# Filling free slots by scatter, moving the first weights, and reordering the tail of attention in a kernel of linear attention and two mixtures of experts

## The chip, the cores and the metric

The kernel runs on one core of a Trainium2 chip. The core has a matrix engine (TensorE, PE), a vector engine (VectorE, DVE), a scalar engine (ScalarE, ACT), a general engine (GpSimd, POOL) and a queue engine (SyncE, SP); each works through its own instructions in order, and semaphores tie them together. SP and POOL also issue the transfers (DMAs). The metric is the device time of one execution in microseconds (us); a kernel's time is the median of its runs.

## The reference

A linear attention with decay (4 batches, 8 heads, 768 steps, head size 48) makes 3072 tokens of width 384. A first mixture of 8 experts (hidden width 1024) sends each token through one expert; a second one does the same for the tokens whose skip score is positive and passes the others through.

```python
for t in range(S):                       # attention
    state = alpha[:, :, t, :, None] * state + einsum('bhd,bhe->bhde', k[:, :, t], v[:, :, t])
    y[:, :, t] = einsum('bhd,bhde->bhe', q[:, :, t], state)
...
e_idx = argmax(x @ w_gate, axis=1)       # first mixture, x: (3072, 384)
for e in range(E):
    mask = e_idx == e
    ye = maximum(x[mask] @ w1[e], 0.0) @ w2[e]
    out[mask] = gate_w[mask, None] * eom[mask, e, None] * ye
...
do_compute = x @ w_skip > 0              # second mixture
out[do_compute] = xc + gate_w[:, None] * (maximum(xc @ w1[e], 0.0) @ w2[e])
```

## The kernel before

**Attention.** The 3072 tokens are 24 chunks of 128 (tiles). A loop over i runs a list of steps (`stages`), each with a lag: at iteration i, a step with lag n works on chunk i + n. Steps of a chunk: `p_scan` (products of the decay along the chunk, DVE), `p_recip` (ACT), `p_k` and `p_q` (k and q scaled by them; the product t on POOL, the rest mostly on DVE), `scores` (PE), `mask` (DVE), `k_back` and `state` (the state S handed on), `y_of` (PE), `x_rows` (PE turns the result into rows of tokens, ACT copies them). The code order sets the order on each engine.

**Routing to experts.** After every four tiles (a group) `gate_logits` computes the gate's logits on PE, `x_route` picks the expert on DVE, and `x_place` ranks the tokens within their expert and writes each token's row (388 floats: 384 values, the weight, the token's number) with an indirect DMA of POOL (a scatter) into a scratch in memory, `scr1`. Expert e owns the rows from e * 3456 on. Groups 0 to 3 put their scatters into a list, from which `x_send` takes one per iteration; group 4's go at once; group 5 is routed and placed inside the first expert's layer 1.

**Free slots.** The first mixture reads 432 rows for every expert, however many tokens it has. So that free rows hold harmless values, `fill_region` (L137) writes a row of zeros with an out-of-range token number into all 432 rows of each expert first: four experts' fills are issued by SP inside the constants, the other four at the end of iteration 0. The scatters of tokens write over them. The constants themselves (`consts`, L111) run on POOL in the lead before the loop.

**Weights.** Each expert's weights come in six pieces of 128x1024, through a buffer of three (`load_piece`, L296). Each half of a piece is split into a high part (ACT, L307) and the rest (DVE, L308), since products are made of three terms. The first expert's pieces are loaded at iterations 4, 7, 10, 13, 16 and 19 and split at 7, 8, 10, 11 and so on to 23.

**Experts.** `stream` (L621) runs the items of `ITEMS` in turn. Item 0 is expert 0 with the rows present before the last group (early rows), item 1 the rest of expert 0, with the rows as the stationary side, items 2 to 8 are experts 1 to 7, and nine more items are the second mixture. An item's `layer1` (L403) makes eight blocks f of the hidden width, `layer2` (L450, L459) eight more; in layer 2 PE already transposes the next item's rows (L359). Steps of the item before (its own routing to `scr2` and its scatters), hooks, weight splits and the loading of the next item's rows (`load_rows`, L340) are woven in between the blocks. `bump` (L207) moves late tokens of expert 0 behind its early rows.

**The seam.** At iteration 22 SP loads expert 0's early rows into two buffers of the weight stage; `first_split`, called from `x_rows` of the last tile, transposes them (L359), splits them, and then the last group's logits follow (L286).

## Time and profile before

| | |
|---|---|
| Time, median of 3 runs (lowest to highest) | 584.15 us (583.17 to 587.17) |
| Profiled execution, its time | 584.72 us |
| Its span, first to last instruction | 582.5 us |
| Busy: PE, DVE, ACT, POOL | 94%, 64%, 53%, 28% |
| Attention (to the first layer 1) | 161.6 us |
| Mean granted clock of PE | 0.966 |

A row of a trace gives the start in us, the duration in us, the engine and line (SPq is SP's queue), the operation, and the tile written and the tiles read; x4 means four of them in a row, and then the duration covers all. In brackets stands how long the engine was idle before, and what ended that. A window's row gives busy time by engine; the share of DMA can pass 1 by a little, since packets overlap.

### The profile page before, as it was taken

What the parts mean: (1) busy time and instruction counts of PE and PEld (TensorE: products, weight loads), DVE (VectorE), ACT (ScalarE), POOL (GpSimd) and SP (SyncE); (2) the same over time, 40 slices, a digit from 0 to 9 for tenths busy, and PEclk for the clock granted to TensorE, in tenths of its full rate; (3) what the DMA queues carried; (4) which work ended last, traced back from release to release, by engine and by line L of the source; (5) the groups of instructions that cost most, each with busy time, mean ns of one, the idle gap of its engine ahead of it and who ended that gap; (6) DMA issues with size and microseconds to landing.
All of it is one profiled execution on the core that took longest, in us unless ns stands there. A gap on an engine that the chain in (4) does not pass through costs nothing.

```text
span 582.5 us, 11777 instructions
## 1 busy us (share of the span) xinstructions
PE 547.2 (94%) x4545; PEld 499.3 (86%) x4545; DVE 375.2 (64%) x867; ACT 309.2 (53%) x723; POOL 164.6 (28%) x171
## 2 busy tenths in 40 slices
PE   5995989897898999999999999999999999999995
PEld 4784777786698899999999999998997999999994
DVE  7997699998264463655546373745546786777850
ACT  3573666765443563645445464636465565566540
POOL 5334255554220320140606041231533011001111
PEclk9697898899889999999999999999999999999999
DMA  8989876331578335272635436162735757666610
GB/s 314 363 309 352 338 259 249 114 112 42 204 259 255 112 88 179 76 261 92 230 128 204 152 126 225 62 222 95 226 124 192 243 194 220 222 217 217 208 68 22
DMA packets 35949, 110.31 MB, mean 189 GB/s; under 512 B 6444, under 2 KB 13228, under 8 KB 35884
## 3 DMA queue, kind: packets, MB, share of 16 engines
q1 hardware_dynamic: 28940, 97.52, 49.0%
q0 software_dynamic: 6944, 11.96, 5.9%
q8 instruction: 37, 0.61, 0.4%
q14 instruction: 28, 0.23, 0.1%
HBM read 88.96 MB, written 27.13 MB: 199 GB/s over the span
## 4 chain that ended last, share of the span: by engine, by line
PE 68%; DVE 15%; DMA 8%; ACT 2%; POOL 2%; issue 2%; SPq 1%; POOLq 0%; DVEq 0%; ACTq 0%
PE ph L403 27%; PE py L450 17%; PE py L459 8%; PE py L403 3%; DVE A L947 3%; DVE P L892 3%; DMA st<-in_w1a_dram 2%; DVE r L917 2%; DMA st<-in_w2b_dram 2%; PE pt L359 2%; PE pt L489 2%; PE ph L421 2%; DVE k L919 1%; DVE qp L928 1%; DMA st<-in_w2a_dram 1%
## 5 line engine op out<-in xcount | busy, mean ns | idle before, releaser
L219 POOL DMA_INDIRECT scr<-x,pi x56 | 67.0, 1197 | 208.9 <-DVE ski L534 83.1
L403 PE MATMUL ph<-xh,w1h 128*128 128x432 f32 (+3 forms) x330 | 110.2, 334 | 0.0
L403 PE MATMUL ph<-xl,w1h 128*128 128x432 f32 (+3 forms) x330 | 106.6, 323 | 0.5 <-DVE xl L364 0.5
L403 PE MATMUL ph<-xh,w1l 128*128 128x432 f32 (+3 forms) x330 | 106.5, 323 | 0.0
L409 DVE SCALAR_TENSOR_TENSOR hl<-ph,hh 128x432 fp32r<-128x432 f32 (+3 forms) x110 | 56.2, 511 | 68.6 <-ACT hh L408 68.1
L308 DVE TENSOR_TENSOR w2l<-st,w2h 128x512 fp32r<-128x512 f32 x96 | 65.0, 694 | 42.9 <-ACT w2h L307 42.7
L408 ACT ACTIVATE hh<-ph 128x432 fp32r<-128x432 f32 (+3 forms) x110 | 50.1, 455 | 79.5 <-PE ph L403 79.3
L307 ACT ACTIVATE w2h<-st 128x512 fp32r<-128x512 f32 x96 | 58.2, 626 | 46.5 <-DMA st<-in_w2a_dram 25.6
L308 DVE TENSOR_TENSOR w1l<-st,w1h 128x512 fp32r<-128x512 f32 x96 | 63.2, 687 | 12.1 <-ACT w1h L307 9.5
L450 PE MATMUL py<-hh,w2h 128*128 128x432 f32 (+1 forms) x192 | 69.0, 359 | 0.0
L450 PE MATMUL py<-hh,w2l 128*128 128x432 f32 (+1 forms) x192 | 67.4, 351 | 0.0
L450 PE MATMUL py<-hl,w2h 128*128 128x432 f32 (+1 forms) x192 | 67.3, 350 | 0.0
L403 PEld LDWEIGHTS ph<-xh,w1h 128*128 128x128 f32 x330 | 62.7, 190 | 2.8 <-issue 1.6
L403 PEld LDWEIGHTS ph<-xl,w1h 128*128 128x128 f32 x330 | 62.5, 190 | 2.4 <-DVE xl L364 0.9
L403 PEld LDWEIGHTS ph<-xh,w1l 128*128 128x128 f32 x330 | 62.8, 190 | 1.1
L307 ACT ACTIVATE w1h<-st 128x512 fp32r<-128x512 f32 x96 | 56.5, 624 | 4.7 <-DMA st<-in_w1a_dram 4.7
L219 POOL DMA_INDIRECT out_dram<-ot,ti x16 | 15.6, 975 | 120.7 <-DVE ot L554 110.3
L459 PE MATMUL py<-w2h,hh 128*128 128x384 f32 (+1 forms) x136 | 48.4, 356 | 0.0
L459 PE MATMUL py<-w2l,hh 128*128 128x384 f32 (+1 forms) x136 | 45.9, 337 | 0.0
L910 POOL TENSOR_TENSOR t<-P,r 112x512 f32<-112x512 f32 x22 | 28.4, 1291 | 58.8 <-DVE P L892 54.1
L459 PE MATMUL py<-w2h,hl 128*128 128x384 f32 (+1 forms) x136 | 43.8, 337 | 0.0
L940 PE MATMUL ps<-qp,k 48*128 48x128 f32 x384 | 31.6, 301 | 7.4 <-POOL hind L134 3.3
(217 smaller groups left out, 1086.2 us busy)
## 6 DMA issues: line engine op xcount, KB each, us to landing
st<-in_w1a_dram SPq DMA_DIRECT2D x24, 512.0 KB, 3.5
st<-in_w2a_dram SPq DMA_DIRECT2D x24, 512.0 KB, 7.6
st<-in_w1b_dram SPq DMA_DIRECT2D x24, 512.0 KB, 3.9
st<-in_w2b_dram SPq DMA_DIRECT2D x24, 512.0 KB, 3.6
x<-in_ad_dram SPq DMA_DIRECT2D x8, 774.0 KB
ain<-in_ad_dram SPq DMA_DIRECT2D x7, 774.0 KB, 5.8
kin<-in_kd_dram SPq DMA_DIRECT2D x7, 768.0 KB
qin<-in_qd_dram SPq DMA_DIRECT2D x7, 768.0 KB, 13.5
```

The costliest lines, as they stand in the source:

```text
L219: ins = nc.gpsimd.indirect_dma_start(out=dst, out_offset=bass.IndirectOffsetOnAxis(ap=idx.bitcast(U32)[0:pp, j:j + 1], axis=0), in_=src, i ...
L307: nc.scalar.activation(out=hi, in_=src, func=AF.Copy)
L308: nc.vector.tensor_tensor(out=lo, in0=src, in1=hi.bitcast(F32), op=ALU.subtract)
L403: nc.tensor.matmul(ph[:, 0:n], w[:, kb, f * 128:(f + 1) * 128], x[:, kb, 0:n], start=(k == 0), stop=(k == 3 * KB - 1),)
L408: nc.scalar.activation(out=hh[:, f, 0:n], in_=ph[:, 0:n], func=AF.Relu)
L409: nc.vector.scalar_tensor_tensor(out=hl[:, f, 0:n], in0=ph[:, 0:n], scalar=0.0, in1=hh[:, f, 0:n].bitcast(F32), op0=ALU.max, op1=ALU.subtract,
L450: nc.tensor.matmul(py[d], w[:, f, dsl], hx[:, f, 0:pp * gg], start=(f == 0 and k == 0), stop=(f == FB - 1 and k == 2),)
L459: nc.tensor.matmul(py[g], hx[:, f, gsl], w[:, f, :], start=(f == 0 and k == 0), stop=(f == FB - 1 and k == 2),)
L892: scans[i] = nc.vector.tensor_tensor_scan(out=P.rearrange("p a b -> p (a b)"), data0=a[0:PR, c].rearrange("p a b -> p (a b)"), data1=floor ...
L910: ti = (nc.gpsimd if i > 1 else nc.vector).tensor_tensor(out=t, in0=P, in1=r, op=ALU.mult)
L940: nc.tensor.matmul(pss[j][:, hp], k2[rr, hp], qp[rr, hp])
L947: nc.vector.tensor_tensor(out=a, in0=ps, in1=causal[:, None, :].to_broadcast([128, NP, C]), op=ALU.mult)
```

## The change

1. Only expert 0's region is filled at the start. Once the counts of all tokens are known (hook in layer 1 of item 0, f = 4), `free_slots` computes on PE and DVE, for each of experts 1 to 7 and each of its 432 rows, the row's address if it is free and an address out of range if it is taken. `fill_free` then issues a scatter of 108 rows of `fill`, four for each expert: for expert 1 in layer 2 of item 0, for expert e in layer 1 (f = 0 to 3) of the item before its own. Three small POOL instructions in `consts` prepare the addresses.
2. The first expert's pieces are loaded at iterations 8, 10, ... 18 and split at iterations 12 to 23, one half each.
3. From tile 18 on, `x_rows` runs one iteration sooner; group 4 is routed and placed one iteration sooner; `y_of` stands ahead of `x_place`; the loop has one iteration fewer; from iteration 20 on `x_send` takes two scatters; `bump` moves to iteration 23; the last group's logits come before `first_split`.
4. Expert 0's early rows are 104x3 = 312 instead of 102x3 = 306, its late rows 120 instead of 126.

```diff
-EARLY1 = 306
+EARLY1 = 312
-    [(True, 0, 0, 102, 3), (True, 0, EARLY1, 126, 1)] + ...
+    [(True, 0, 0, 104, 3), (True, 0, EARLY1, 120, 1)] + ...
...
+        si = sp.tile([128, E, G1], I32, name="si", bufs=1)
+        nc.gpsimd.iota(si, pattern=[[CAP, E], [1, G1]], base=0, channel_multiplier=G1)
+        nc.gpsimd.tensor_copy(slote, si)
+        nc.gpsimd.tensor_copy(slot, slote[:, 0])
...
+    def free_slots():
+        cnt = sp.tile([128, E], F32, name="cntf")
+        pm = psM.tile([128, 512], F32, name="smp")
+        nc.tensor.matmul(pm[:, 0:E], onesb, ohs1)
+        nc.vector.tensor_copy(cnt, pm[:, 0:E])
+        used = sp.tile([128, E, G1], F32, name="used", bufs=1)
+        nc.vector.tensor_tensor(out=used, in0=slot..., in1=cnt..., op=ALU.is_lt)
+        idx = sp.tile([128, E * G1], I32, name="fidx", bufs=1)
+        nc.vector.scalar_tensor_tensor(out=idx..., in0=used, scalar=BIG, in1=slote, op0=ALU.mult, op1=ALU.add)
+    def fill_free(e, g):
+        scatter(scr1[:, :], slots["at"], e * G1 + g, fill[0:P1, :], P1, E * CAP - 1, "a")
...
             rows_copy(pt, x_t[g], j)
-            if i == NTILE - 1:
-                first_split()
             if j == GT - 1:
                 sm_t[g] = psM.tile([128, 512], F32, name="smp")
                 lt_t[g] = gate_logits([xt_t.pop(g * GT + u) for u in range(GT)], sm_t[g])
+            if i == NTILE - 1:
+                first_split()
...
-            if to_send:
-                to_send.pop(0)()
+            for _ in range(2 if i >= early else 1):
+                if to_send:
+                    to_send.pop(0)()
...
-            (p_recip, 3), (scores, 0), (mask, 0), (x_place_0, -4), (state, -1), (x_route_1, -3), (p_k, 2), (p_q, 2),
-            (k_back, 0), (x_send, 0), (x_place_1, -3), (x_route_0, -3), (p_scan, 4), (y_of, -1), (x_rows, -2),
+            (p_recip, 3), (scores, 0), (mask, 0), (x_place_0, -4), (state, -1), (x_route_1, -2), (p_k, 2), (p_q, 2),
+            (k_back, 0), (x_send, 0), (y_of, -1), (x_place_1, -2), (x_route_0, -3), (p_scan, 4), (x_rows_0, -2), (x_rows_1, -1),
...
-            (p_k, 1), (constants, FILL), (p_scan, 3),
+            (p_k, 1), (constants, 1), (p_scan, 3),
...
-        for i in range(NTILE + 2):
-            if i == early_at + 1:
-                bump(ohs1, ecl1, sm_t[NTILE // GT - LATE - 1][0:1, 400:401], EARLY1)
+        for i in range(NTILE + 1):
...
-                if fn is p_scan and 6 <= i < 24 and i % 3:
-                    split_half(w_cur, (i - 6) // 3, i % 3 - 1, pieces[(i - 6) // 3])
+                if fn is p_scan and 12 <= i < 24:
+                    split_half(w_cur, (i - 12) // 2, i % 2, pieces[(i - 12) // 2])
...
-            if i == 0:
-                fill_region(scr1, P1, G1, FILL)
-            if 4 <= i and i % 3 == 1 and (i - 4) // 3 < 6:
-                pieces.append(load_piece(w1a, w2a, 0, (i - 4) // 3, stp))
+            if 8 <= i and i % 2 == 0 and (i - 8) // 2 < 6:
+                pieces.append(load_piece(w1a, w2a, 0, (i - 8) // 2, stp))
+            if i == NTILE - 1:
+                bump(ohs1, ecl1, sm_t[early // GT - 1][0:1, 400:401], EARLY1)
...
+    at(todo, 0, 4, free_slots)
+    for e in range(1, E):
+        for g in range(G1):
+            at(todo2 if e == 1 else todo, 0 if e == 1 else e, g + (e == 1), lambda e=e, g=g: fill_free(e, g))
```

**Where instructions move.** SP's queue behind the first loads of inputs, before (ain, kin, qin and vin are buffers of the attention's inputs, scr_77 is `scr1`, st a weight piece):

```order
L1094 DMA wg2s<-in_wg_dram 128x96
L140 DMA scr_77<-fill 432x1x388 x4
L879 DMA ain_114<-in_ad_dram 128x1548
L879 DMA kin_117<-in_kd_dram 128x1536
L879 DMA qin_120<-in_qd_dram 128x1536
L140 DMA scr_77<-fill 432x1x388 x4
L883 DMA vin_123<-in_vn_dram 128x1152
L879 DMA ain_115<-in_ad_dram 128x1548
L879 DMA kin_118<-in_kd_dram 128x1536
L879 DMA qin_121<-in_qd_dram 128x1536
L296 DMA st<-in_w1a_dram 128x1024
L883 DMA vin_124<-in_vn_dram 128x1152
```

and with the change:

```order
L1124 DMA wg2s<-in_wg_dram 128x96
L145 DMA scr_77<-fill 432x1x388
L907 DMA ain_116<-in_ad_dram 128x1548
L907 DMA kin_119<-in_kd_dram 128x1536
L907 DMA qin_122<-in_qd_dram 128x1536
L911 DMA vin_125<-in_vn_dram 128x1152
L907 DMA ain_117<-in_ad_dram 128x1548
L907 DMA kin_120<-in_kd_dram 128x1536
L907 DMA qin_123<-in_qd_dram 128x1536
L911 DMA vin_126<-in_vn_dram 128x1152
L907 DMA ain_118<-in_ad_dram 128x1548
L907 DMA kin_121<-in_kd_dram 128x1536
```

One fill is left of the eight, the inputs of the next chunks follow it at once, and the first weight piece stands further down.

DVE at iteration 7, the first with a split before (P is the scan, A the mask of two score tiles, w1l the lower part of a weight half):

```order
L917 TENSOR_TENSOR r<-kin_117,r 112x512
L919 SCALAR_TENSOR_TENSOR k_817<-t,r 112x512
L892 SCALAR_TENSOR_TENSOR P<-ain_114,floor 112x516
L308 TENSOR_TENSOR w1l_194<-st,w1h_193 128x512
L947 TENSOR_TENSOR A<-ps,causal 128x512 x2
L979 TENSOR_TENSOR S<-pu,S 112x192
```

and with the change:

```order
L945 TENSOR_TENSOR r<-kin_119,r 112x512
L947 SCALAR_TENSOR_TENSOR k_814<-t,r 112x512
L920 SCALAR_TENSOR_TENSOR P<-ain_116,floor 112x516
L975 TENSOR_TENSOR A<-ps,causal 128x512 x2
L1007 TENSOR_TENSOR S<-pu,S 112x192
L945 TENSOR_TENSOR r<-kin_119,r 112x512
```

The subtraction of the split is gone from this place; it comes back from iteration 12 on.

DVE in the tail, before: the last steps of k and q, the mask of chunk 22 (A), the state, and then the routing of group 4 (mxa to ls):

```order
L917 TENSOR_TENSOR r<-kin_118,r 112x512
L919 SCALAR_TENSOR_TENSOR k_2057<-t,r 112x512
L928 TENSOR_TENSOR qp<-qin_121,P 112x512
L947 TENSOR_TENSOR A<-ps,causal 128x512 x2
L979 TENSOR_TENSOR S<-pu,S 112x192
L148 TENSOR_REDUCE mxa<-smp 128x4
L151 TENSOR_TENSOR dla<-smp,mxa 128x32
L160 SCALAR_TENSOR_TENSOR eqa<-dla,w_84 128x32
L164 TENSOR_REDUCE rka<-eqa 128x4
L166 TENSOR_TENSOR oha<-w_84,rka 128x32
L245 TENSOR_TENSOR lo<-smp,oha 128x32
L247 TENSOR_REDUCE ls<-lo 128x4
```

and with the change, from the mask of chunk 21 on:

```order
L975 TENSOR_TENSOR A<-ps,causal 128x512 x2
L1007 TENSOR_TENSOR S<-pu,S 112x192
L153 TENSOR_REDUCE mxa<-smp 128x4
L156 TENSOR_TENSOR dla<-smp,mxa 128x32
L165 SCALAR_TENSOR_TENSOR eqa<-dla,w_84 128x32
L169 TENSOR_REDUCE rka<-eqa 128x4
L171 TENSOR_TENSOR oha<-w_84,rka 128x32
L250 TENSOR_TENSOR lo<-smp,oha 128x32
L252 TENSOR_REDUCE ls<-lo 128x4
L945 TENSOR_TENSOR r<-kin_120,r 112x512
L947 SCALAR_TENSOR_TENSOR k_2100<-t,r 112x512
L956 TENSOR_TENSOR qp<-qin_123,P 112x512
```

The routing now stands ahead of r, k and qp of the last chunk, one mask sooner; the placing (not shown) follows them.

## Rows read from the trace of the kernel before

**Rows 1.** The page's first line: span and instructions.
```profile
span 582.5 us, 11777 instructions
```

**Rows 2.** Windows: us; busy PE, PEld, DVE, ACT, POOL; clock, DMA share, GB/s.
```profile
17.50:54.50 37.00, 30.83 (x441) 25.57 (x437) 35.52 (x63) 21.98 (x64) 10.89 (x12) 0.87 0.94 327
54.50:63.14 8.64, 7.92 (x82) 6.66 (x84) 1.25 (x3) 2.13 (x8) 3.99 (x3) 0.61 1.02 419
63.14:129.50 66.36, 61.56 (x919) 50.51 (x917) 63.96 (x133) 47.64 (x142) 33.50 (x28) 0.95 0.55 202
...
199.09:428.35 229.26, 229.26 (x1416) 213.00 (x1415) 125.88 (x325) 117.49 (x231) 63.94 (x55) 1.00 0.47 158
```

**Rows 3.** Order of time, DVE: start, us, engine, line, operation [idle <-releaser].
```profile
63.14 0.69 DVE L308 TENSOR_TENSOR w1l<-st,w1h 128x512 fp32r<-128x512 f32 x1 [7.39 <-ACT w1h L307]
```

**Rows 4.** Chain that ended last, 0 to 66 us: start, us, what.
```profile
48.29 14.16 DMA st<-in_w1a_dram
```

**Rows 5.** Order of time, SP's queue, 15 to 41 us.
```profile
15.92 9.62 SPq L140 DMA_DIRECT2D scr<-fill  x4
...
30.43 9.91 SPq L140 DMA_DIRECT2D scr<-fill  x4
```

**Rows 6.** Order of time, POOL, the constants.
```profile
10.30 0.32 POOL L120 IOTA ti<- 128x72 int32 x1
...
11.16 0.92 POOL L124 CAST w<-ei 128x8 f32<-128x8 int32 x1
```

**Rows 7.** Order of time, DVE, behind the constants.
```profile
17.57 0.69 DVE L917 TENSOR_TENSOR r<-kin,r 112x512 f32<-112x512 f32 x1 [1.12 <-POOL t L910]
```

**Rows 8.** Order of time, DVE, tail of attention.
```profile
134.89 1.40 DVE L308 TENSOR_TENSOR w2l<-st,w2h 128x512 fp32r<-128x512 f32 x1 [0.20 <-ACT w2h L307]
...
136.21 1.27 DVE L947 TENSOR_TENSOR A<-ps,causal 128x512 f32<-128x512 f32 x2
...
140.28 1.29 DVE L947 TENSOR_TENSOR A<-ps,causal 128x512 f32<-128x512 f32 x2 [0.61 <-PE ps L940]
...
141.75 0.18 DVE L148 TENSOR_REDUCE mxa<-smp 128x4 f32<-128x32 f32 x1
...
144.47 0.69 DVE L308 TENSOR_TENSOR w2l<-st,w2h 128x512 fp32r<-128x512 f32 x1
```

**Rows 9.** Order of time, POOL, tail of attention.
```profile
134.28 1.46 POOL L910 TENSOR_TENSOR t<-P,r 112x512 f32<-112x512 f32 x1 [0.77 <-DVE k L919]
...
144.54 1.48 POOL L219 DMA_INDIRECT scr<-x,pi  x1 [6.08 <-DVE osa L202]
```

**Rows 10.** Order of time, SP's queue, expert 0's early rows.
```profile
152.44 0.68 SPq L340 DMA_DIRECT2D st<-scr  x2
```

**Rows 11.** Order of time, PE, from attention to layer 1.
```profile
158.38 0.43 PE L359 MATMUL ps<-ident,st 102*128 102x102 f32 x1 [0.35 <-DMA st<-scr]
...
159.76 1.94 PE L286 MATMUL smp<-xt,wg1s 112*32 112x128 f32 x32
...
161.62 0.62 PE L403 MATMUL ph<-xh,w1h 128*128 128x306 f32 x1
```

**Rows 12.** Chain that ended last, in order of time, 126 to 205 us.
```profile
165.49 1.27 PE py L403 x9
...
173.34 4.04 DMA scr<-x,pi
...
201.20 1.76 PE ph L403 x9
```

**Rows 13.** Order of time, PE, first transposes of items 1 to 3.
```profile
182.39 0.38 PE L376 MATMUL pt<-ident,xr 126*128 126x126 f32 x2
...
196.37 0.53 PE L359 MATMUL pt<-ident,xr 108*128 108x108 f32 x4
...
223.98 0.53 PE L359 MATMUL pt<-ident,xr 108*128 108x108 f32 x4
```

**Rows 14.** Order of time, POOL, last scatter of item 0's results to the output.
```profile
204.25 1.08 POOL L219 DMA_INDIRECT out_dram<-x,ski  x1 [0.30 <-issue]
```

More of the change, by code (lines that the diff above doesn't have):

```diff
@@ L42 @@
 LW = 32
-EARLY1 = 306
+EARLY1 = 312
 EARLY2 = 128
-FILL = 4
 ITEMS = (
-    [(True, 0, 0, 102, 3), (True, 0, EARLY1, 126, 1)] + [(True, e, 0, P1, G1) for e in range(1, E)]
+    [(True, 0, 0, 104, 3), (True, 0, EARLY1, 120, 1)] + [(True, e, 0, P1, G1) for e in range(1, E)]
     + [(False, 0, 0, 128, 1), (False, 0, EARLY2, 128, 1)] + [(False, e, 0, P2, G2) for e in range(1, E)]
@@ L290, in gate_logits @@
         return take_logits(sm_ps, GT, 128)
+    slots = {}
+    def free_slots():
[4 more added lines that the diff above has]
+        used = sp.tile([128, E, G1], F32, name="used", bufs=1)
+        nc.vector.tensor_tensor(
+            out=used, in0=slot[:, None, :].to_broadcast([128, E, G1]), in1=cnt[:, :, None].to_broadcast([128, E, G1]),
+            op=ALU.is_lt,
+        )
+        idx = sp.tile([128, E * G1], I32, name="fidx", bufs=1)
+        nc.vector.scalar_tensor_tensor(
+            out=idx.rearrange("p (e g) -> p e g", e=E), in0=used, scalar=BIG, in1=slote, op0=ALU.mult, op1=ALU.add
+        )
+        slots["at"] = idx
+    def fill_free(e, g):
+        scatter(scr1[:, :], slots["at"], e * G1 + g, fill[0:P1, :], P1, E * CAP - 1, "a")
     def load_piece(w1, w2, e, i, stp):
@@ L698, in stream @@
                     xr_n = load_rows(nxt)
+                for fn in hooks2.get((m, f), ()):
+                    fn()
                 if f == 0 and nxt:
@@ L1060, in among @@
             return run
-        rest = NTILE - GT * (LATE + 1)
+        rest, early = NTILE - GT * (LATE + 1), NTILE - GT * LATE
         x_route_0, x_place_0 = (among(fn, 0, rest) for fn in (x_route, x_place))
-        x_route_1, x_place_1 = (among(fn, rest, NTILE) for fn in (x_route, x_place))
+        x_route_1, x_place_1 = (among(fn, rest, early) for fn in (x_route, x_place))
+        x_rows_0, x_rows_1 = among(x_rows, 0, early - 2), among(x_rows, early - 2, NTILE)
         causal = cp.tile([128, C], F32, name="causal")
@@ L1204, with at @@
     checks = [m for m, it in enumerate(ITEMS) if m > 1 and not in_rows(it)][0:2 * B]
[L1205 to L1212 removed]
+    todo, todo2 = {}, {}
+    def at(where, m, f, fn):
+        where.setdefault((m, f), []).append(fn)
+    at(todo, 0, 0, lambda: x_route(last))
+    at(todo, 0, 2, lambda: x_place(last))
+    at(todo, 0, 4, free_slots)
+    for e in range(1, E):
+        for g in range(G1):
+            at(todo2 if e == 1 else todo, 0 if e == 1 else e, g + (e == 1), lambda e=e, g=g: fill_free(e, g))
+    for h, m in enumerate(checks):
+        at(todo, m, 0, lambda h=h: load_decay(h))
+        at(todo, m, 4, lambda h=h: check_decay(h))
+    n_it = len(ITEMS)
+    for m, f, fn in (
+        (n_it - 6, 3, judge_decay), (n_it - 5, 3, judge_sums), (n_it - 4, 2, lambda: judge_most(0)),
+        (n_it - 4, 6, lambda: judge_most(1)), (n_it - 3, 3, judge_all),
+    ):
+        at(todo, m, f, fn)
+    stream(w_cur, "b", "o", (xe, xc, x_first), todo, todo2)
     ectx.close()
```

14 lines of the change are left out of this document (4 added, 10 removed).

## The prediction

> **What bounds the kernel now.** I read the windows by stage first, then the order of time on VectorE (DVE), then the queues that DVE was found waiting for, and last the seam between attention and the first expert. The profiled execution took 584.72 us with a span of 582.5 us [rows 1]; the median of the three runs is 584.15 us, 0.57 us less. The sum below is made against 584.72 and then lowered by 0.57.
>
> Up to about 130 us DVE sets the pace: 35.5 of 37.0 us busy from 17.5 to 54.5 us, 64.0 of 66.4 us from 63.1 to 129.5 us. Between these two lies a hole: 1.25 us busy out of 8.64, while the DMA engines are at 1.02 of their share and move 419 GB/s [rows 2]. The hole is one wait: DVE stands 7.39 us before the first subtraction of the weight split (L308), because ScalarE (ACT) has no high part to give it [rows 3]. The chain says why: the weight piece issued at 48.29 us needed 14.16 us to land [rows 4]. In SP's queue ahead of it stand two blocks of four fills of the scratch, and SP was occupied 9.62 and 9.91 us with issuing them [rows 5]. After the attention stage the expert stages belong to TensorE (PE): in the window from 199 to 428 us PE is busy all the time and DVE 126 of 229 us [rows 2]. So a part of the change pays if it shortens DVE's row up to 130 us, the seam, or PE's stream; work on other engines costs only where it makes these wait.
>
> **The change part by part.**
>
> *Fills and first weights, one item.* Seven of eight fills leave the SP queue, 7 x 432 rows x 388 x 4 bytes = 4.7 MB, at 419 GB/s [rows 2] 11 us of transfers. The first split moves from iteration 7 to iteration 12, the first load of a piece from iteration 4 to iteration 8. DVE has the same 12 subtractions as before, so nothing is saved on work; the wait of 7.39 us goes. What would be late next is the scores of the same chunk: PE had been held by the same full queues (values of v) and now isn't. I take -7.4 us. Bounds: 0 (another transfer holds DVE for as long) and -8.1 (the subtraction leaves this place too, but comes back later).
>
> *Constants.* POOL runs three more small instructions (iota, cast, copy) ahead of its first product t. DVE waits for that product, 1.12 us already [rows 7], so all of it is on the path. Rows of such instructions: an iota of 128x72 took 0.32 us, a cast of 128x8 0.92 us [rows 6]. Three at 0.32 to 0.92 make 1.0 to 2.8 us; the iota is like the first row, the cast like the second, the copy has four elements and no row of its own. I take +1.2 us.
>
> *Tail of attention.* Before, group 4 (tiles 16 to 19) is routed after the mask of chunk 22; now after that of chunk 21, and placed once r, k and q of chunk 23 are made. In the rows: the mask of chunk 21 starts at 136.21; with S, r, k and q it lasts until 139.67 (140.28 less the 0.61 of waiting); routing and placing take 2.72 us (141.75 to 144.47) [rows 8]. In the new order the first scatter of the group can go at 136.21 + 3.46 + 2.72 = 142.4 instead of 144.54 [rows 9]: 2.1 us sooner. One subtraction fewer stands before that point (8 splits instead of 9 ahead of the mask of chunk 20), 0.69 us [rows 8]. Together 2.8 us. From this scatter hang the four scatters, the loading of expert 0's early rows (issued at 152.44 [rows 10], used up to 158.38), their transposes, and layer 1 at 161.62 [rows 11]. The loads have the same bytes within 2% and I leave their 5.94 us as they are. Before, the logits of the last group (L286, 159.76 to 161.62, 1.86 us) stand behind those transposes on PE [rows 11]; now they stand ahead, where PE has nothing else to do but wait for the load: 1.86 us less. Sum -2.8 - 1.9 = -4.7 us. Bounds: -1.9 (PE, not DVE, sets the tail, and only the logits move) and -6.6 (the load gets faster too, rival 1).
>
> *104x3 instead of 102x3.* Expert 0's early rows are 312 columns instead of 306. Nine products of 306 columns took 1.27 us, nine of 432 1.76 us [rows 12]: 0.43 ns a column. 144 products (72 in each layer) x 6 x 0.43 ns = +0.4 us. The second item has 120 rows instead of 126; there the rows are the stationary side, so nothing is gained.
>
> *Free slots by scatter.* PE gets one small product (at most one of those above, 0.14 us) and DVE three small instructions: +0.2 us. POOL gets 28 scatters. Each group of four stands ahead of the load of its expert's rows, and the first four also wait for the loading of expert 0's late rows, which PE used at 182.39 [rows 13]. Four at 1.3 us, the last landing 4.04 us after its start [rows 12]: 182.4 + 3.9 + 4.0 = 190.3. The load then takes as long as that at 152.44, 5.9 us: 196.2, and PE wants it at 196.37 [rows 13]. It just fits; the load is larger, so I take +0.3 (0 to +2). For expert 2 POOL is free at 205.33 [rows 14]; its fills land by 213.8, with the load 219.7, and PE wants it at 223.98 [rows 13]. For experts 3 to 7 POOL is idle when its fills come. Nothing there.
>
> A possible cost on DVE: beside POOL's product t at 134.28 one subtraction took 1.40 us instead of 0.69; but beside the scatter at 144.54 the subtraction at 144.47 took 0.69 [rows 8, 9]. So scatters, unlike products, do not stretch it, and with DVE busy for 126 of 229 us [rows 2] I take nothing. The Trainium skill (GPSIMD Engine Reference, Key points) says that POOL shares its SBUF interfaces with DVE and contends with instructions of two SBUF inputs; taken for every POOL instruction, that speaks against 28 more of them. By it, 28 x 0.7 us = 20 us of DVE time in the expert stages, and still none on PE's path; the row of the product agrees with the page, the row of the scatter does not show it.
>
> **Sum:** -7.4 + 1.2 - 4.7 + 0.4 + 0.2 + 0.3 = -10.0 us. 584.72 - 10.0 = 574.7 in a profile, 574.2 as a median: **574.2 us**, 1.7% faster. About 1% (5.8 us) is what a measurement of this kernel can tell from no change; faster than that means under 578.3.
>
> **The rivals.**
>
> 1. *The load of the early rows is shorter.* It is the one transfer of the tail that everything waits for. For 306 rows of 1552 bytes, 475 kB, 5.94 us are long: at 419 GB/s [rows 2] they would take 1.1 us. If 104 rows are spread over more of the DMA engines, it may come down to the 4.04 us in which a scatter of 128 such rows landed [rows 12]: 1.9 us less, 574.2 - 1.9 = 572.3. For it: the long time for few bytes. Against: four scatters have only just landed, and latency is the same for any shape. The Trainium skill (DMA: Bandwidth & Descriptors, Why a DMA increments its semaphore by 16 and not by 1) states that a DMA uses the largest number of engines up to 16 that divides its slowest dimension. By this 102 rows run on 6 engines and 104 on 13; the row agrees in that it is long, but no row here counts engines.
>
> 2. *The tail gives only the logits.* PE's chain scores, state, y, rows of each chunk becomes the bound once DVE's routing is out of its way, and the early load comes no sooner: -1.9 instead of -4.7, 577.0. For it: DVE waited 0.61 us for PE at the mask of chunk 22 [rows 8]. Against: before that DVE was 64.0 of 66.4 us busy [rows 2].
>
> 3. *The change does not free the queue.* The pieces come in pairs of iterations now (8 to 18) and 3 MB of them meet the inputs of later chunks; DVE waits again, at iteration 12, for as long: 574.2 + 7.4 = 581.6. Against: DMA share 0.55 in the window 63.1 to 129.5 [rows 2], and four iterations from load to first split.
>
> 4. *Slower: the fills by scatter come late.* With s for one scatter (1.3 us in the sum), the first four make PE wait 4 x (s - 1.3) us, those of expert 2 make it wait from s = 2.4 on, 4 x (s - 2.4). Both together cancel the gain of 10.0 at s = 3.1 us, and give 590 at s = 3.9 us. What could do it: most indices of a fill lie beyond the bound and are dropped, and dropping might cost more than writing. Against: the scatters to the output drop rows in the same way, and one of them took 1.08 us [rows 14].
>
> **How the numbers follow.** Forecast 574.2: 0.52, with a range of its own of 572.5 to 577 from the bounds of the constants (-0.2, +1.6) and of the first fills (-0.3, +1.7). Rival 1 572.3 (570.5 to 574): 0.20. Rival 2 577.0 (575 to 579): 0.14. Rival 3 581.6: 0.08. Rival 4 590 or more: 0.06. The range 570.5 to 579 holds the first three up to their edges and leaves out rivals 3 and 4 and a little of the others: about 8 in 10. Faster by over 1% (under 578.3): nearly all of the first two, most of rival 2, 0.83. Within 1%: rival 3 and the rest of rival 2, 0.12. Slower by over 1%: most of rival 4, 0.05.
>
> **What would show it.** Right: no wait of DVE for a weight split before 130 us; DVE's wait for the first product t of POOL about 1.2 us longer than 1.12; the scatters of group 4 start some 9 us earlier than 144.54 (7.4 - 1.2 + 2.8), layer 1 of expert 0 some 11 us earlier than 161.62; L286 ahead of the transposes of the early rows; from there on, distances to layer 1 as before. Wrong: a new wait of DVE or ACT for a weight piece in iterations 12 to 23; the rows of experts 1 to 7 waited for by PE; scatters of the fills of over 2 us each; the early load landing in 4 us or less (rival 1).

## The result, and the profile after

The changed kernel takes 578.71 us (median of 4 runs, 578.34 to 578.98), the kernel before, in the same rounds, 584.88 us (583.17 to 587.17): ratio 0.9892, 95% interval 0.9855 to 0.9928, 6.2 us faster. Forecast were 574.2 us, a gain of 10.0 us. The profiled execution took 578.34 us with a span of 576.6 us, 5.9 us under that of before [rows 1].

Four points in the order of time show where the difference arises. Each is the start of an instruction, us from the span's start:

| | before | after | moved | forecast |
|---|---|---|---|---|
| last scan of attention (chunk 23) | 129.50 | 123.29 | -6.2 | -6.2 (hole -7.4, constants +1.2) |
| layer 1 of expert 0 | 161.62 | 155.56 | -6.1 | -10.9 (tail -4.7) |
| last matmul of the program | 574.87 | 566.81 | -8.1 | -10.0 (+0.9 for columns, free slots, rows) |
| end of the span | 582.5 | 576.6 | -5.9 | -10.0 |

So the hole came out as forecast. The tail gave nothing. The expert stages gave 2.0 us that nobody had counted, and behind the last matmul 2.2 us were lost.

**The hole.** Windows of the changed kernel (columns as in [rows 2]), and below it SP's queue:

```profile
55.40:61.27 5.87, 5.14 (x72) 4.04 (x70) 4.58 (x8) 3.71 (x11) 3.83 (x3) 1.00 0.21 79
```
```profile
16.79 1.00 SPq L145 DMA_DIRECT2D scr<-fill  x1
17.91 0.44 SPq L907 DMA_DIRECT2D ain<-in_ad_dram  x1
...
48.55 0.53 SPq L322 DMA_DIRECT2D st<-in_w1a_dram  x1
```

From one scan to the next (55.40 to 61.27) it is 5.87 us; before, the two scans at the same place began 54.52 and 67.14, 12.62 us apart, with the wait of [rows 3] between. DVE waits for no weight split there, nor anywhere before 132 us. One fill is left in the queue, 1.00 us instead of 9.62 [rows 5], and the inputs follow it. The constants cost 0.88 us: DVE's first r starts at 18.45 instead of 17.57 [rows 7]:

```profile
18.45 0.69 DVE L945 TENSOR_TENSOR r<-kin,r 112x512 f32<-112x512 f32 x1 [1.72 <-POOL t L938]
```

**The tail.** PE, in order of time, from the ranks of group 3 to the scores of chunk 21 (the state's products left out); then DVE and ACT in the same stretch:

```profile
117.05 0.18 PE L190 MATMUL smp<-ecap,onesb 1*128 1x32 bf16 x1 [1.99 <-DVE lo L250]
...
119.37 1.97 PE L1022 MATMUL py<-A,vin 128*64 128x128 f32 x16
121.27 1.01 PE L278 MATMUL pxt<-ident,xt 112*128 112x112 f32 x4
123.00 1.01 PE L278 MATMUL pxt<-ident,xt 112*128 112x112 f32 x4 [0.72 <-ACT x L283]
123.94 2.08 PE L968 MATMUL ps<-qp,k 48*128 48x128 f32 x16
...
127.91 1.97 PE L1022 MATMUL py<-A,vin 128*64 128x128 f32 x16
129.81 1.29 PE L1028 MATMUL py<-qp,S 48*48 48x128 f32 x16
131.79 0.60 PE L278 MATMUL pxt<-ident,xt 112*128 112x112 f32 x4 [0.70 <-ACT xt L1030]
132.33 1.08 PE L291 MATMUL smp<-xt,wg1s 112*32 112x128 f32 x32
133.34 1.16 PE L968 MATMUL ps<-qp,k 48*128 48x128 f32 x16
```
```profile
126.05 1.29 DVE L975 TENSOR_TENSOR A<-ps,causal 128x512 f32<-128x512 f32 x2 [0.95 <-PE ps L968]
...
132.29 0.69 DVE L334 TENSOR_TENSOR w2l<-st,w2h 128x512 fp32r<-128x512 f32 x1 [2.76 <-ACT w2h L333]
134.53 1.29 DVE L975 TENSOR_TENSOR A<-ps,causal 128x512 f32<-128x512 f32 x2 [1.54 <-PE ps L968]
```
```profile
131.14 0.60 ACT L1030 ACTIVATE xt<-py 112x512 f32<-112x512 f32 x1 [1.97 <-PE py L1028]
131.64 0.62 ACT L333 ACTIVATE w2h<-st 128x512 fp32r<-128x512 f32 x1
```

Before, the mask of chunk 20 started at 131.22, those of chunks 21 and 22 at 136.21 and 140.28 [rows 8]. Now they start at 126.05, 134.53 and 141.16: the first is 5.2 us sooner, the third 0.9 us later. DVE waits 0.95 and 1.54 us for scores, and 2.76 us for a high part of the weights that ACT makes only after xt. In PE's row the scores of chunk 21 (133.34) stand behind y of chunk 19, the transposes of chunk 19's rows, which wait 0.70 us for ACT's xt, and the logits. That order is what the change wrote. It also put the rows of two chunks (121.27 and 123.00) ahead of the scores of chunk 20. The granted clock in this stretch is 0.50, which is 1.2 GHz (windows of the changed kernel; the second row is for the expert stages below):

```profile
117.00:130.30 13.30, 12.53 (x108) 10.14 (x109) 11.38 (x24) 7.62 (x24) 9.20 (x7) 0.50 0.14 51
155.56:160.56 5.00, 5.00 (x38) 4.56 (x38) 3.39 (x13) 2.07 (x7) 0.00 (x0) 1.00 1.06 339
```

The scatter of group 4 (144.54 before [rows 9]) starts 3.9 us sooner, and the load of the early rows (152.44 [rows 10]) 2.7 us sooner. Measured from the last scan both are later than before: the scatter comes 17.3 us behind it instead of 15.0, the load 26.5 us instead of 22.9. POOL, SP's queue and PE of the changed kernel, in order of time:

```profile
140.62 1.48 POOL L224 DMA_INDIRECT scr<-x,pi  x1 [8.89 <-DVE osa L207]
...
153.63 0.61 POOL L1056 COPY xc<-st 104x4 f32<-104x4 f32 x3 [7.45 <-DMA st<-scr]
```
```profile
149.77 0.78 SPq L366 DMA_DIRECT2D st<-scr  x2
```
```profile
153.55 1.08 PE L291 MATMUL smp<-xt,wg1s 112*32 112x128 f32 x32
154.56 0.49 PE L385 MATMUL ps<-ident,st 104*128 104x104 f32 x3
...
155.56 0.41 PE L429 MATMUL ph<-xh,w1h 128*128 128x312 f32 x1
```

The load has landed by 153.63, at most 3.86 us after its issue, where 102 rows took 5.94 [rows 10, 11]. The logits now stand ahead of the transposes as intended, and layer 1 follows the load's issue after 5.8 us instead of 9.2. These 3.4 us pay back the 3.5 us by which the load came late.

**The expert stages and the end.** In the first 5 us of layer 1 the clock was granted at 0.79 before and is 1.00 now, which by an estimate is worth 5 x 0.21 = 1.05 us, since PE is busy all of that time; PE's longest wait for the high part of the second item's rows fell from 1.5 to 0.7 us. Together 1.85 of the 2.0 us. No run varies these two alone, and rows_behind_scores below, whose clock is 1.00 there too, is only 0.7 us shorter than before from layer 1 to the last matmul (412.54 against 413.25). The window before, and PE's waits from layer 1 to the end, before and after (us in total, times, longest):

```profile
161.62:166.62 5.00, 5.00 (x32) 4.88 (x28) 1.83 (x9) 1.25 (x4) 0.00 (x0) 0.79 0.99 295
```
```profile
PE ph L421 <- ACT xh L377: 1.7, 2, 1.5
```
```profile
PE ph L447 <- ACT xh L403: 0.9, 2, 0.7
```

The fills by scatter take 1.1 us each, not the 3 us that a slower outcome needed, and PE waits no longer for experts' rows than before. Their whole sum is 30.4 us on POOL, which has time (group's row of the changed kernel):

```profile
L224 POOL DMA_INDIRECT scr<-fill,fidx x28 | 30.4, 1085 | 24.6 <-DVE w2l L334 9.0 <-DMA xr<-scr 7.7 <-issue 7.6
```

The last rows of the two kernels are alike, the last scatter 1.3 us behind the last matmul; yet the span ends 7.6 us behind that matmul before (582.5 less 574.87) and 9.8 us after (576.6 less 566.81). POOL's last row, before and after:

```profile
576.14 0.97 POOL L219 DMA_INDIRECT out_dram<-ot,ti  x1 [3.22 <-DVE ot L554]
```
```profile
568.08 0.97 POOL L224 DMA_INDIRECT out_dram<-ot,ti  x1 [3.22 <-DVE ot L580]
```

### The profile page after: what moved, and what is told of

Its sections match the earlier page's. It is cut to its first block, busy times and chain, and to the rows that moved or that the text cites. A ratio compares the mean times of both kernels' runs of the same rounds, so it can differ in the third digit from the quotient of the medians.

```text
span 576.6 us, 11837 instructions
## 1 busy us (share of the span) xinstructions
PE 545.9 (95%) x4546; PEld 498.3 (86%) x4546; DVE 374.5 (65%) x870; ACT 309.3 (54%) x723; POOL 195.7 (34%) x202
## 4 chain that ended last, share of the span: by engine, by line
PE 69%; DVE 17%; DMA 5%; ACT 4%; issue 3%; POOL 1%; SPq 0%; POOLq 0%; DVEq 0%; ACTq 0%
PE ph L429 27%; PE py L476 17%; PE py L485 10%; DVE A L975 3%; DVE P L920 3%; PE py L429 3%; DVE r L945 2%; PE pt L385 2%; PE pt L515 2%; DMA st<-in_w1a_dram 2%; DVE qp L956 2%; DVE k L947 2%; PE ph L447 1%; PE smp L505 1%; DMA st<-in_w2b_dram 1%
## 5 line engine op out<-in xcount | busy, mean ns | idle before, releaser
L224 POOL DMA_INDIRECT out_dram<-x,ski x32 | 35.5, 1110 | 9.7 <-issue 9.1
```

Source lines behind the costliest of these rows:

```text
L224: ins = nc.gpsimd.indirect_dma_start(out=dst, out_offset=bass.IndirectOffsetOnAxis(ap=idx.bitcast(U32)[0:pp, j:j + 1], axis=0), in_=src, i ...
```

## Theories and experiments

*Theory A*: the reordered tail leaves PE idle at group 3 (y no longer covers DVE's routing), the clock falls to 1.2 GHz for 13 us, and that eats the gain. *Theory B*: the order of PE's own queue does it (rows and logits ahead of the next scores), whatever the clock; the splits of weights in each iteration, on ACT and DVE, add to it. *Theory E*: the length of the end depends on the branch around code that this data never takes. All runs below were timed beside the kernel before (median 586.0 to 586.3 us there), so the ratios are what is compared. Points from the profiles:

| kernel | ratio (95%) | last scan | early load issued | layer 1 | scan to layer 1 | last matmul | behind it |
|---|---|---|---|---|---|---|---|
| before | 1 | 129.50 | 152.44 | 161.62 | 32.12 | 574.87 | 7.6 |
| after | 0.9892 (0.9855-0.9928) | 123.29 | 149.77 | 155.56 | 32.27 | 566.81 | 9.8 |
| hole_only | 0.9881 (0.9852-0.9909) | 123.12 | 146.34 | 155.46 | 32.34 | 568.55 | 10.7 |
| tail_only | 1.0111 (1.0070-1.0152) | 129.28 | 154.58 | 160.52 | 31.24 | 572.54 | 17.4 |
| y_behind_scan_until_18 | 0.9889 (0.9860-0.9918) | 122.97 | 148.91 | 154.72 | 31.75 | 566.62 | 9.8 |
| busy_at_group3 | 0.9869 (0.9834-0.9905) | 126.08 | 149.25 | 156.93 | 30.85 | 566.62 | 9.9 |
| rows_behind_scores | 0.9815 (0.9777-0.9854) | 122.97 | 144.19 | 150.40 | 27.43 | 562.94 | 9.8 |
| rows_and_fill2 | 0.9810 (0.9773-0.9847) | 125.22 | 146.35 | 152.66 | 27.44 | 563.72 | 9.8 |
| rows_102 | 0.9870 (0.9823-0.9918) | 123.59 | 144.60 | 151.53 | 27.94 | 567.35 | 10.6 |
| logits_first | 0.9893 (0.9863-0.9924) | 122.95 | 147.73 | 154.45 | 31.50 | 567.86 | 10.4 |
| fills_by_sync | 1.0110 (1.0062-1.0157) | 128.60 | 154.57 | 160.35 | 31.75 | 575.87 | 16.9 |
| weights_as_before | 0.9888 (0.9850-0.9926) | 123.37 | 148.16 | 153.30 | 29.93 | 566.17 | 9.8 |
| after_no_slow_path | 0.9807 (0.9767-0.9847) | 121.91 | 147.72 | 153.67 | 31.76 | 565.95 | 6.3 |
| before_no_slow_path | 0.9923 (0.9881-0.9965) | | | | | | 5.5 |

**hole_only and tail_only: which part pays?** hole_only is the change without its third and fourth parts; tail_only is these two parts alone. The list of steps is as in the first line in hole_only, as in the second in tail_only:

```diff
-            (k_back, 0), (x_send, 0), (x_place_1, -3), (x_route_0, -3), (p_scan, 4), (y_of, -1), (x_rows, -2),
+            (k_back, 0), (x_send, 0), (y_of, -1), (x_place_1, -2), (x_route_0, -3), (p_scan, 4), (x_rows_0, -2), (x_rows_1, -1),
```

> The kernel before with the first two parts of the change alone: free slots of experts 1 to 7 filled by scatter, first weights loaded from iteration 8 and split from iteration 12; the tail of attention and the early rows (102 x 3) as before. Theory A (the reordered tail gives nothing until layer 1 starts, since y ahead of the routing leaves TensorE waiting for group 3's one-hot and its clock then falls for some 13 us): the last scan ends about 6.2 us sooner, layer 1 starts at about 155.4 us as in the changed kernel, TensorE's long half-clock stretch from 117 to 130 us is absent, and the time is 577.5 to 579.5 us. The sum on record (hole -7.4, constants +1.2, free slots +0.2, expert 1's rows +0.3, and the tail, not in here, worth -4.7): 579.2 us, and then the changed kernel, 0.5 us from it, lost the tail's 4.7 us elsewhere.

> The kernel before with the third part alone: tail reordered, early rows 104 x 3; fills all by SyncE at the start and weights loaded from iteration 4 as before. Sum on record: 584.9 - 4.7 + 0.4 = 580.6 us. Theory A: the wait of the rank matmul for DVE's one-hot grows here too (3.5 us before, 6.3 us in the changed kernel, over all groups), the granted clock falls to half ahead of iteration 20, and the time is 583 to 586 us. If the tail reordering works here as summed and fails in the changed kernel, it is the weight splits in every iteration from 12 to 23 that take its gain (theory B).

hole_only starts layer 1 at 155.46 us, 0.10 us from the changed kernel, and has its time. So the whole reordered tail, with the 104 rows, is worth nothing there, and the gain of the change is the hole. tail_only shortens scan to layer 1 by 0.9 us, not by 4.7, and is slower than the kernel before: its last matmul is 2.3 us sooner, but 17.4 us lie behind it.

**y_behind_scan_until_18 and busy_at_group3: is it the clock?**

```diff
+        y_of_0, y_of_1 = among(y_of, 0, early - 2), among(y_of, early - 2, NTILE)
...
-            (k_back, 0), (x_send, 0), (y_of, -1), (x_place_1, -2), (x_route_0, -3), (p_scan, 4), (x_rows_0, -2), (x_rows_1, -1),
+            (k_back, 0), (x_send, 0), (y_of_1, -1), (x_place_1, -2), (x_route_0, -3), (p_scan, 4), (y_of_0, -1), (x_rows_0, -2), (x_rows_1, -1),
```
```diff
...
-            (p_recip, 3), (scores, 0), (mask, 0), (x_place_0, -4), ...
+            (p_recip, 3), (busy, -4), (scores, 0), (mask, 0), (busy, -4), (x_place_0, -4), ...
```

> The changed kernel, but y of chunks 0 to 17 is computed where it was before (behind the scan, after the routing); from chunk 18 on it stands ahead of the routing as in the change. Theory A: TensorE has y(17) to do while DVE routes group 3, so its wait for that one-hot falls from 1.99 us to under 1 us, the granted clock stays at 1.00 through 117 to 130 us, layer 1 starts 3 to 4.5 us sooner (151 to 152.5 us) and the time is 574.2 to 575.7 us. Theory B (rows at lag -1 wait for their own copy, and weight splits of every iteration sit ahead of it on ACT, whatever the clock): 578.2 to 579.2 us, as the changed kernel.

> The changed kernel with 2 x 24 bf16 matmuls of 96 columns added on TensorE in iteration 19 (ahead of the scores and ahead of the ranks of group 3) into unused columns of the routing's PSUM tile: nothing else moves. They fill the two waits of 1.24 and 1.99 us there. Theory A: the granted clock does not fall at 117 us, the scores and y of chunks 19 to 21 run at full rate, layer 1 starts 2 to 4.5 us sooner, time 574.5 to 576.7 us. Theory B: as the changed kernel or up to 2 us later, 578.5 to 580.7 us.

Both cut the slow stretch: to 6.8 us at 0.52 in the first and 3.7 us at 0.57 in the second (one window of each, then the second kernel from its last scan to layer 1, and the mask of chunk 21 on DVE in the first).

```profile
122.50:129.30 6.80, 6.80 (x58) 5.62 (x60) 5.72 (x9) 3.35 (x10) 5.16 (x5) 0.52 0.22 79
```
```profile
118.50:122.20 3.70, 3.66 (x41) 3.29 (x41) 1.91 (x3) 1.48 (x4) 2.17 (x2) 0.57 0.36 139
126.08:156.93 30.85, 25.87 (x409) 20.96 (x408) 17.27 (x46) 17.57 (x54) 11.58 (x14) 1.00 0.36 125
```
```profile
133.68 1.29 DVE L975 TENSOR_TENSOR A<-ps,causal 128x512 f32<-128x512 f32 x2 [1.54 <-PE ps L968]
```

Yet DVE still waits 1.54 us for the scores of chunk 21, which are masked at 133.68, and scan to layer 1 falls only by 0.5 and 1.4 us. In busy_at_group3 the last scan itself came 2.8 us later, which took that back. From the last scan to layer 1 the granted clock is 0.89 in the changed kernel, 0.90 in the first of the two and 1.00 in the second; so the first took away the part of the slow stretch ahead of the last scan, and the second is the test. Theory A fell: with the full clock over the whole of that way, 1.4 us of the missing 4.8 came back.

**rows_behind_scores: is it PE's order?**

```diff
-            (p_recip, 3), (scores, 0), (mask, 0), (x_place_0, -4), ...
+            (p_recip, 3), (scores, 0), (x_rows_1, -2), (mask, 0), (x_place_0, -4), ...
...
-            ..., (p_scan, 4), (x_rows_0, -2), (x_rows_1, -1),
+            ..., (p_scan, 4), (x_rows_0, -2),
...
-        for i in range(NTILE + 1):
+        for i in range(NTILE + 2):
```

> The changed kernel, but from chunk 18 on the rows (transposes, copies, logits) come one iteration later, right behind the next scores on TensorE, instead of ahead of them; so no scores wait for a copy of the same iteration, and iteration 19 has one chunk's rows, not two. What the first four runs left standing (theory B, the order of TensorE's queue): DVE no longer waits 0.9 and 1.5 us for the scores of chunks 20 and 21, the mask of chunk 21 starts at 129 to 131 us instead of 134.5, layer 1 starts at 151.5 to 153.5 us instead of 155.6. Whether that reaches the end: expert 1's first weights land 9.9 us after their issue behind the fills of the second scratch and hold item 1's first layer at 178.5 to 179 us in all runs so far, so that most of the gain is lost there; last matmul 565 to 566 us instead of 566.8, the time 0 to 2 us below the changed kernel, 7 to 8.5 us below the kernel before. Rival (nothing holds item 1 but TensorE): the whole 2 to 4 us arrive, 8.5 to 10.5 us below the kernel before. Rival (the order is not it): mask of chunk 21 later than 133 us, no gain.

PE and DVE in order of time, iterations 20 and 21, and the window from the last scan to layer 1:

```profile
126.15 1.08 PE L1028 MATMUL py<-qp,S 48*48 48x128 f32 x16
127.16 1.16 PE L968 MATMUL ps<-qp,k 48*128 48x128 f32 x16
128.34 0.60 PE L278 MATMUL pxt<-ident,xt 112*128 112x112 f32 x4
128.87 1.08 PE L291 MATMUL smp<-xt,wg1s 112*32 112x128 f32 x32
```
```profile
128.84 1.35 DVE L334 TENSOR_TENSOR w2l<-st,w2h 128x512 fp32r<-128x512 f32 x1 [0.68 <-ACT w2h L333]
130.12 1.27 DVE L975 TENSOR_TENSOR A<-ps,causal 128x512 f32<-128x512 f32 x2
```
```profile
122.97:150.40 27.43, 24.80 (x399) 20.17 (x398) 17.61 (x46) 15.87 (x50) 11.46 (x14) 1.00 0.35 119
```

The scores of chunk 21 now follow y at once (127.16), their mask starts at 130.12 without a wait for them, and layer 1 at 150.40, 27.43 us behind the last scan: 4.7 us less than before, the sum on record to a tenth. That close a match is chance: on this way the granted clock is 1.00 now and was 0.87 before, and 104 rows instead of 102 are worth 0.5 us of it (rows_102 below); neither was in that sum. Time 574.74 us (573.07 to 576.40), ratio 0.9815: faster than both kernels; its interval ends where that of the changed kernel begins. Against busy_at_group3, whose clock from the last scan to layer 1 is 1.00 as well, 3.4 us remain that the clock cannot explain; they belong to the moved rows and logits. The expected second gate, expert 1's weights holding the second item at 178.5 us, was wrong: it starts its layer 1 at 173.2.

**rows_and_fill2: the fills of the second scratch.** The eight fills ahead of expert 1's weights in SP's queue move into iterations 13 to 20:

```diff
+            if 13 <= i < 21:
+                fill_region(scr2, P2, G2, i - 13, i - 12)
...
-    fill_region(scr2, P2, G2)
```

> As rows_behind_scores, and the eight fills of the second scratch are issued one per iteration from 13 to 20 of attention instead of ahead of expert 1's weights. If expert 1's weights behind those fills are the second gate: they land some 4 to 6 us sooner, item 1's first layer starts at 174 to 175.5 us instead of 178.9 (about 22.2 us after layer 1 began, which is TensorE's own work there), last matmul at 562 to 563.5 us, time 9.5 to 12 us below the kernel before. If TensorE alone sets it, this kernel and rows_behind_scores agree within 0.7 us. If the fills disturb attention's loads, the last scan ends later than 124 us and the gain is gone.

Layer 1 to the last matmul became 1.5 us shorter (411.06 instead of 412.54), but the times agree within 0.3 us. Its profiled execution was 2.3 us late at the last scan, and already at the scan of 51.26 (49.23), before the first of those fills. Whether the fills are worth moving stays open.

**rows_102: the price of the early load.**

```diff
-    [(True, 0, 0, 104, 3), (True, 0, EARLY1, 120, 1)]
+    [(True, 0, 0, 102, 3), (True, 0, EARLY1, 126, 1)]
```

> rows_behind_scores with the early rows as 102 x 3 (306 columns) again instead of 104 x 3. In the traces the load of 102 rows a partition group lands 5.9 us after its issue (152.44 to 158.38 before, 146.34 to 152.21 in hole_only), that of 104 in at most 3.65 us (144.19 to 147.84 in rows_behind_scores), where TensorE asks for it at 149.39. If the load's length is now the gate: issue at about 144.2, last piece at about 150.1, TensorE waits 0.5 to 1 us for it, transposes of 102 rows as before, layer 1 starts 0.5 to 1.3 us later (150.9 to 151.7 us), time 0 to 1.3 us above rows_behind_scores. Rival (312 or 306 columns and the load make no difference on the path): the same start within 0.3 us.

PE at the seam, the chain that ended last, and PE at the first layer 2:

```profile
149.01 1.08 PE L291 MATMUL smp<-xt,wg1s 112*32 112x128 f32 x32
...
150.71 0.31 PE L385 MATMUL ps<-ident,st 102*128 102x102 f32 x1 [0.29 <-DMA st<-scr]
```
```profile
152.54 11.63 DMA st<-in_w1a_dram
```
```profile
166.07 0.41 PE L476 MATMUL py<-hh,w2h 128*128 128x306 f32 x1 [2.27 <-DVE hl L435]
```

The last piece is used at 150.71, 6.1 us after its issue at 144.60, and PE waits 0.29 us for it; scan to layer 1 is 0.5 us longer, the lower end of what was expected. The median is 3.8 us above rows_behind_scores (intervals overlap). The rest is lost behind layer 1: expert 1's first weights, issued at 152.54, land 11.63 us later, and PE waits 2.27 us for a low part that DVE makes behind their split. That the load of 102 rows caused this is not shown. The Trainium skill (DMA: Bandwidth & Descriptors, Why a DMA increments its semaphore by 16 and not by 1) says that the number of engines is the largest up to 16 that divides the slowest dimension. 5.9 to 6.1 us for 102 rows against at most 3.9 for 104 agree with it; no row counts engines.

**logits_first: the logits alone,** on hole_only:

```diff
+            if j == GT - 1:
+                sm_t[g] = psM.tile([128, 512], F32, name="smp")
+                lt_t[g] = gate_logits([xt_t.pop(g * GT + u) for u in range(GT)], sm_t[g])
             if i == NTILE - 1:
                 first_split()
-            if j == GT - 1:
-                sm_t[g] = psM.tile([128, 512], F32, name="smp")
-                lt_t[g] = gate_logits([xt_t.pop(g * GT + u) for u in range(GT)], sm_t[g])
```

> hole_only with one piece of the tail's reordering: the logits of the last group ahead of the transposes of the early rows on TensorE (and 102 x 3 as before). On record this piece was worth 1.9 us: TensorE then works on the logits while the load of the early rows lands (last piece at 152.2 us in hole_only) and starts layer 1 right behind the transposes, at 153.4 to 153.8 us instead of 155.46; time 1 to 2 us below hole_only. Rival: the logits wait for the last chunk's rows, which wait for the same copy, and the start moves by under 0.5 us.

Scan to layer 1 fell by 0.8 us, not 1.9; the time did not move (0.9893 against 0.9881). The logits run while the load lands, as said, but at the full clock they last 1.0 us and not the 1.9 that [rows 11] shows (the clock granted there, from 159.76 to 161.62, is 0.50), and the load, issued 1.4 us later in this execution, is then the gate (PE, in order of time):

```profile
149.91 1.08 PE L291 MATMUL smp<-xt,wg1s 112*32 112x128 f32 x32
152.44 0.40 PE L385 MATMUL ps<-ident,st 102*128 102x102 f32 x2 [1.45 <-DMA st<-scr]
153.62 0.31 PE L385 MATMUL ps<-ident,st 102*128 102x102 f32 x1 [0.79 <-DMA st<-scr]
```

**fills_by_sync and weights_as_before: what closed the hole?**

```diff
...
-            (p_k, 1), (constants, 1), (p_scan, 3),
+            (p_k, 1), (constants, 4), (p_scan, 3),
...
+            if i == 0:
+                fill_region(scr1, P1, G1, 4)
...
```
```diff
-                if fn is p_scan and 12 <= i < 24:
-                    split_half(w_cur, (i - 12) // 2, i % 2, pieces[(i - 12) // 2])
+                if fn is p_scan and 6 <= i < 24 and i % 3:
+                    split_half(w_cur, (i - 6) // 3, i % 3 - 1, pieces[(i - 6) // 3])
...
-            if 8 <= i and i % 2 == 0 and (i - 8) // 2 < 6:
-                pieces.append(load_piece(w1a, w2a, 0, (i - 8) // 2, stp))
+            if 4 <= i and i % 3 == 1 and (i - 4) // 3 < 6:
+                pieces.append(load_piece(w1a, w2a, 0, (i - 4) // 3, stp))
```

> The changed kernel with all eight regions filled by SyncE at the start as before, no free_slots, no fills by scatter, no slot constants; weights from iteration 8 and splits from 12 as in the change. Tells which of the two edits removes DVE's wait of 7.39 us at 63.14 us. If the later split alone does (by iteration 12 the weights have long landed): no wait for a weight split, the last scan at 122 to 124 us as in the changed kernel (123.29), the constants' 0.9 us gone, time within 1 us of the changed kernel, 5 to 7 us below the kernel before. If the fills' 4.6 MB and 19.5 us of SyncE's queue do: a wait of 3 us or more stays, or moves to an input load, and the last scan is at 126 us or later.

> The changed kernel with the first weights loaded from iteration 4 and split from iteration 7 as before; fills by scatter as in the change. If the free queue alone removes the hole: without the seven fills the first piece of weights lands some 5 us after its issue at about 48 us instead of 14 us, DVE does not wait for its split, last scan at 122.5 to 124.5 us, time within 1 us of the changed kernel. If only the later split does: DVE waits 3 to 7 us near 60 us, last scan at 126 us or later, time 2.5 to 6 us above the changed kernel.

DVE and PE of fills_by_sync at the old hole, PE of the kernel before at the same place, and SP's queue of weights_as_before, in order of time:

```profile
61.70 1.29 DVE L971 TENSOR_TENSOR A<-ps,causal 128x512 f32<-128x512 f32 x2 [5.78 <-PE ps L964]
```
```profile
56.37 0.31 PE L999 MATMUL pu<-vin,kn 128*64 128x48 f32 x1 [7.24 <-DMA vin<-in_vn_dram]
```
```profile
55.22 0.31 PE L975 MATMUL pu<-vin,kn 128*64 128x48 f32 x1 [6.26 <-DMA vin<-in_vn_dram]
```
```profile
34.41 0.43 SPq L322 DMA_DIRECT2D st<-in_w1a_dram  x1
```

With the fills in SP's queue and the split moved, DVE waits 5.78 us at the same place, now for scores, because PE had waited 7.24 us for v. That wait was there before too (6.26 us at 55.22), hidden behind the wait for weights. So the later split alone gave 0.9 us at the last scan. With the queue freed and the weights as before, the first piece is issued at 34.41 instead of 48.29, DVE waits there neither for a split nor for scores, and the last scan starts within 0.1 us of the changed kernel's. The fills' leaving closed the hole; moving the weights was not needed. In the tail the old splits are even 2.3 us better (29.93 against 32.27), but the last matmul is only 0.6 us sooner and the time is the same. The granted clock on that way is 0.94 there and 0.89 in the changed kernel, so the 2.3 us are not the splits' alone; how much of the tail's loss the splits of every iteration add to PE's order, no run separates.

**before_no_slow_path and after_no_slow_path: the end.** Left out are the branch behind the last item and the register load that decides it, with the recurrence and overflow passes in it:

```diff
-    rany = nc.values_load(
...
-    with tc.If(rany > 0):
...
```

> The kernel before without the branch at the end (the sequential recurrence and the overflow passes, which this data never takes) and without the register load that decides it: left out are those passes. In the traces 8.0 us lie between the start of the last kind of matmul group and the end of the span before, 10.1 us in the changed kernel, 11.0 and 17.7 us in two experiments, with nothing but small transfers in them. Theory E (the length of that end is set by the branch over code that isn't taken and differs from kernel to kernel by where the code lies): without the branch it is 5 to 7 us in this kernel and in the changed one alike, and the time here is 1 to 3 us below the kernel before. Rival (the end is set by the last scatter and the closing of queues): 8 us as before, no difference.

> The changed kernel with the same branch and register load left out. Theory E: the same length of the end as in before_no_slow_path within 0.5 us, so that the two differ by what the last matmul shows, 7.5 to 8.5 us, instead of the 5.9 us of the spans with the branch; 9 to 11 us below the kernel before. Rival: its end stays at 10 us and the two differ by 6 us.

(The expectations count from a product 0.35 us ahead of the last matmul.) Behind the last matmul 5.5 and 6.3 us are left, instead of 7.6 and 9.8. So of the 2.2 us that the changed kernel loses there, 1.4 go with the branch and its load; 0.7 stay unexplained, a little more than the 0.5 us that theory E allowed. The profiled execution of before_no_slow_path was 3 us late at the last scan already (132.55), so only its end is read. By their ratios the two are 4.5 and 11.3 us below the kernel before, 6.8 apart, which the intervals do not tell from 6.2. The Trainium skill (Runtime: NRT & Kernel Launch, Instruction fetch mechanics) says that a taken branch to code outside the two loaded pages must fetch it first. The rows agree in that the end is shorter without the branch, and in the queues named "instruction": they carry five packets there with the branch and one without (tail_only behind 572 us, then after_no_slow_path behind its last matmul; packets, MB, share):

```profile
q14 instruction: 4, 0.03, 0.7%
q8 instruction: 1, 0.02, 0.5%
```
```profile
q14 instruction: 1, 0.01, 0.5%
```

But these packets are not what makes one end longer than another. In all fourteen kernels the last packet of any queue comes 5.0 to 5.8 us behind the last matmul. What differs is the stretch behind it, in which no engine and no queue has a row: 0.5 and 1.2 us without the branch, 2.1 us in the kernel before, 4.5 in the changed one, 11.6 in the two kernels that combine SyncE's fills with the new tail. What runs in it, no run shows.

## Why the prediction was right and wrong

The time lies inside the stated range of 570.5 to 579, but at its upper edge, where it had been given to rival 2 (575 to 579); it misses the forecast's own range of 572.5 to 577. (From the bounds named for it, that range comes to 573.7 to 577.5.) Three terms went wrong by 2 to 5 us, and one of them took back part of the other two: without the 2.9 us by which the expert stages beat the sum the time would have been 581.6. So the number is in part luck, and the reasons are told term by term.

*Hole and constants (-7.4 + 1.2)*: right, size and cause (about -7.1 and +0.9). The last scan moved by 6.21 us. The item lumped fills and weights; the runs give it to the fills alone. The remark that PE's wait for v would be late next, and was freed by the same queue, is what fills_by_sync shows.

*Tail (-4.7)*: the step that failed. It costed DVE's row only: "the first scatter of the group can go at 136.21 + 3.46 + 2.72", as if the scores came in time. But rows and logits had been moved ahead of the scores in PE's queue, and each now waits for ACT's copy of the same iteration. DVE, never idle for long in the rows read, got waits of 0.95, 2.76 and 1.54 us in two iterations. Counted from the last scan, the group's first scatter came 2.3 us later instead of 2.8 sooner, and the early load 3.5 us later. Rival 2 (PE's chain becomes the bound) had this mechanism at 0.14, and its bound of -1.9 was still too good: until layer 1 the tail gave +0.15. With the rows behind the scores this stretch is 4.8 us shorter than in the changed kernel: 3.4 us at an equal clock, which is the order, and 1.4 us that go with the clock, for which the sum had no term.

*Logits (-1.9, part of the tail)*: right in place, wrong in size; the 1.86 us had been read at half clock, at full clock it is 1.0.

*Rival 1 (the load gets shorter)*: true of the load (at most 3.9 us instead of 5.94), but in the changed kernel PE, not the load, was last, so it gave no time of its own there; rows_102 prices it at 0.5 us until layer 1. The argument against it, that latency is the same for any shape, does not hold for this load: 5.9 to 6.1 us with 102 rows, at most 3.9 with 104.

*Rivals 3 and 4*: did not happen; no wait for the pieces at iteration 12, fills at 1.1 us. DVE did wait for splits again behind 132 us, 2.76, 2.51 and 2.10 us, but for ACT's high part and not for a piece; the last two stand in rows_behind_scores as well (2.51 and 2.08), which is faster.

*Columns, free slots, rows of expert 1 (+0.9)*: covered by the 2.0 us by which the expert stages got shorter, not seen one by one.

*The end*: not in the sum. 2.2 us were lost behind the last matmul. Misses: tail 4.85, end 2.16, stages -2.9, together the 4.1 us between the forecast gain and the profiled one.

## What to carry to other kernels

A moved step must be costed in every queue it passes: here the gain was on DVE's row, and the loss came from what stood ahead of the next scores on PE, whose row had not been read there. Put work that waits for another engine behind what the bounding engine asks for next, even if that work is the one to be hurried. When a wait is removed, look which other transfer landed at the same time: the split and v were late together, and emptying their common queue, not the later split, removed both waits.

## What was not expected of the hardware

The end of a program of nearly the same code lasted 7.6, 9.8, 10.4 to 10.7 and 16.9 to 17.4 us behind the same last matmul, alike in kernels of one family; without the branch it lasted 5.5 and 6.3 us. The difference lies in a stretch behind the last packet (2.1 to 11.6 us with the branch) that shows in no row of an engine or a queue. In tail_only it cost 9.7 us where the last matmul had gained 2.3.
